# Scores by source parity, a transposed value sum, block-diagonal states, gate sums at odd tokens, and a new order

## The chip, the cores and the metric

One core of a Trainium2 chip runs the kernel. The metric is the device time of one execution in microseconds (us). The engines are TensorE (PE in the profile, with PEld for its weight loads), VectorE (DVE), ScalarE (ACT), GpSimd (POOL) and SyncE (SP), which here only issues transfers. Matmul results go to PSUM, which the kernel uses as eight banks of 128 x 512 float32; everything else lies in SBUF.

## What is computed

A gated linear attention over 4 batches, 8 heads, 768 tokens and head size 48, then a two-layer network over all 3072 tokens (384 to 2048 and back) with g = h * cos(h) in between.

```
f = 1.0 / (1.0 + np.exp(-f_logit))
for t in range(S):
    state = f[:, :, t, :, None] * state + np.einsum('bhd,bhe->bhde', k[:, :, t], v[:, :, t])
    y[:, :, t] = np.einsum('bhd,bhde->bhe', q[:, :, t], state)
x = np.ascontiguousarray(attn_out.transpose(0, 2, 1, 3)).reshape(B * S, H * D)
h = x @ w_in
g = h * np.cos(h)
return (g @ w_out).astype(np.float32)
```

## The kernel before

**Tiling.** The tokens are cut into 12 *pairs* of 256 tokens, n = 0 to 11, three pairs to a batch. In a pair, partition p holds two neighbouring tokens, the even one (e = 0) and the odd one (e = 1). The two halves of 64 partitions, g = 0 and 1, are two chunks of 128 tokens. Heads go in two groups of four, u = 0 and 1.

**Steps.** `describe` makes a graph of named steps; the number behind a name is the pair, and what follows the dot is a part of it:

- f, k, q, v: loads. ex and ln (ACT): softplus of -f_logit, the negative logarithm of the gate.
- cum (PE, L335 to L341): sums of it along the tokens of a chunk, once for each head group, for even and odd tokens alike (a 384-column matmul, two of 192 columns, one of them with a strict triangle as weights) and the chunk's total (four tiny matmuls). eb and ei (ACT): exponentials of minus and plus the sum.
- qm, km (L363, POOL or DVE): q times eb and k times ei. Both go through a transpose to qkt: pairs 0 to 3 on PE (tq, tk, L391, with the copy qkt), pairs 4 to 11 by a transposing DMA on SP's queue (tq, L380).
- sc (PE, L411): scores. The output's partitions are the source tokens of one parity x in the chunks g = 0 and 1, its columns the 128 targets. am (DVE, L415): mask.
- ps (PE, L434): the sum of k times v over a chunk. st (DVE, L449) adds the state that was carried, sz (L456) multiplies by the chunk's decay. The state is a tile of [128, 4, 2, 48] in which only the own half of the rows is filled, so that one matmul serves two heads.
- y (PE, L473): masked scores times v, a matmul for each head, parity and chunk, which contracts 64 tokens, with the scores as weights. yi (PE, L483): q times the state, added in the same PSUM.
- yb (copy), tx (PE, L505: three transposes), xe (copy): y is turned, so that x has the 384 features on partitions.
- vb: v in bf16. w, wc: weights loaded and cast to bf16, staged in the slots of g.
- h (PE, L531): first layer, for 128 tokens in units 0 and 1 and for 256 in units 2 to 12; co (ACT, L536): cosine; g (DVE, L513): product; o (PE, L547): second layer; ot: copy; out: store.
- zf (PE, L257): matmuls of zeros, which compute nothing.

**What sets the order.** `ORDER` (L34 to L110) is written out: every word is a step with its engine letter (T PE, S ACT, V DVE, G POOL, Y SP) and the slots of its tiles or PSUM banks. `emit` issues the steps in this order. Each engine runs its own steps in the order of the list and waits for the data. An activation of another kind than the one before costs a table load on ACT (L536, L586). `SLOTS` gives the number of buffers of each kind of tile.

Of the kernel before, what the change touches and what calls it, by code (L numbers as in the profile page):

```python
# [9 lines left out]
F32 = mybir.dt.float32  # L10
BF16 = mybir.dt.bfloat16
AF = mybir.ActivationFunctionType
HALF_PI = math.pi / 2.0

B, H, S, D = 4, 8, 768, 48
C = 128
# [4 lines left out]
HD = H * D  # L21
NQ = DF // 512
# [5 lines left out]
SLOTS = {"f": 3, "k": 3, "q": 3, "v": 3, "sp": 3, "b": 3, "bi": 3, "qk": 3, "vb": 3, "qkt": 5, "am": 4,  # L28
         "sz": 4, "st": 2, "yb": 4, "x": 4, "g": 5, "co": 4, "ot": 4}
WITHIN = 12  # L30
ZEROS = 24
# [3 lines left out]
zf0:T0 zsz.2:V zsp.2:V zqk.2:V zsp.0:V f0.1:S0 zf19:T1 zf21:T0 zf4:T4 zf18:T5 zf15:T4 zf11:T5  # L35
f1.0:S1 f0.0:S zqk.0:V zf8:T4 ex0.1:S ex1.0:S f1.1:Y zf17:T5 k0.1:Y0 ln1.0:S2 cum1.0:T2 eb1.0:S0
ln0.1:S0 cum0.1:T3 ex1.1:S k0.0:Y ex0.0:S ln0.0:S q1.0:Y0 qm1.0:G2 ln1.1:S ei0.1:S0 v0:Y0 tq1.0:T6
km0.1:V0 eb0.1:S1 k1.0:Y1 ei1.0:S1 km1.0:V zf14:T7 zf10:T1 cum0.0:T7 ei0.0:S km0.0:V tk1.0:T
cum1.1:T0 eb1.1:S qkt1.0:V0 q0.1:Y1 qm0.1:G eb0.0:S tk0.1:T1 f2:Y2 tq0.1:T qkt0.1:V1 q0.0:Y ex2:S
ln2:S0 q1.1:Y vb0:G0 ps0.1:T4,5 sc1.0:T2 am1.0:V0 ps0.0:T sc0.1:T6 am0.1:V1 tk0.0:T1 k1.1:Y qm0.0:G  # L40
tq0.0:T cum2.1:T2 sz0.00:V2 qm1.1:G ei1.1:S cum2.0:T qkt0.0:S2 sz0.01:V km1.1:G w0.0:Y0 wc0.0:G
zf6:T6 tq1.1:T7 tk1.1:T qkt1.1:S3 sc0.0:T0 sc1.1:T6 ei2:S2 eb2:S2 st0.1:V0 am0.0:V2 yi0.1:T4 zf12:T5
am1.1:V3 zf16:T0 sz0.10:V2 zsz.3:G v1:Y1 vb1:G1 sz0.11:V y0.0:T5 y0.1:T y1.1:T1,0 yb0.0:S0
ps1.0:T2,3 ps1.1:T y1.0:T yb0.1:V1 tx0.1:T6 w0.1:Y1 zf7:T7 yi1.0:T w0.2:Y2 tx0.0:T7 xe0.1:S0
st1.0:V1 h1.00:T4 sz1.00:V3 yb1.0:S2 zf20:T2 xe0.0:S sz1.01:V yi1.1:T w0.3:Y3 zf1:T1 w1.3:Y4 wc0.1:V
wc0.2:V k2:Y2 yb1.1:S3 zf2:T2 st1.1:V0 sz1.11:V2 wc0.3:V h1.01:T co1.0:S0 q2:Y2 zf13:T2 h0.10:T6
tx1.1:T1 wc1.3:G xe1.1:S1 sz1.10:G g1.0:V0 zqk.1:V km2.1:G0 qm2.1:G h0.01:T2 tx1.0:T0 h0.00:T
xe1.0:S qm2.0:G co0.0:S1 km2.0:G g0.0:V1 h0.11:T co0.1:S2 g0.1:V h1.10:T0 w1.2:Y2 h1.11:T co1.1:S3
h2.31:T4 h2.30:T co2.3:S0 h2.10:T2 h2.11:T h2.21:T6 g1.1:V tq2.1:T0 w1.1:Y3 wc1.1:G g2.3:V4 h2.20:T
co2.1:S1 tq2.0:T1 v2:Y2 g2.1:V wc1.2:V f3:Y0 o3.3:T4 tk2.1:T o1.3:T5 h2.01:T2 h2.00:T co2.2:S2  # L50
tk2.0:T g2.2:V co2.0:S3 qkt2.0:V4 w1.0:Y2 vb2:G2 wc1.0:G o1.2:T qkt2.1:S1 v3:Y0 g2.0:V o0.1:T6
o0.2:T ps2.1:T7 ps2.0:T sc2.0:T0 sc2.1:T2 st2.0:V1 o3.2:T o0.3:T ex3:S o1.1:T k3:Y0 am2.1:V2
am2.0:V1 sz2.01:V3 q3:Y1 f4:Y1 ln3:S2 yi2.0:T7 cum3.1:T2 sz2.00:G cum3.0:T o3.1:T ei3:S0 y2.1:T0
y2.0:T eb3:S1 f5:Y2 o0.0:T km3.1:V2 v4:Y1 km3.0:G qm3.1:G zf22:T1 q5:Y0 yb2.0:V1 vb3:S0 v5:Y2
tx2.0:T7 xe2.0:S2 yi2.1:T ps3.0:T1,2 ps3.1:T q4:Y2 qm3.0:V yb2.1:S0 sz3.00:V2 sz3.01:V tk3.0:T3
tq3.0:T qkt3.0:V2 ot0:S0 tk3.1:T7 out0:Y ex4:S tx2.1:T0 xe2.1:V o1.0:T ln4:S0 tq3.1:T ex5:S h3.11:T0
q6:Y1 ln5:S2 st3.1:V0 qkt3.1:V0 ot1:V1 o3.0:T ot3:V2 sz3.11:V3 sc3.1:T2 sc3.0:T6 k4:Y1 am3.1:V3
h3.10:T co3.1:S0 h3.30:T4 h3.31:T out1:Y am3.0:V0 co3.3:S1 g3.1:V3 h3.20:T2 f6:Y0 y3.0:T6,7 y3.1:T
yb3.0:S3 v6:Y0 yi3.1:T h3.21:T yb3.1:S2 k5:Y2 co3.2:S2 sz3.10:V h3.00:T0 tx3.1:T6 xe3.1:S3 h3.01:T
g3.3:V co3.0:S3 tx3.0:T7 xe3.0:V vb4:G1 g3.2:V cum4.1:T4 cum4.0:T ei4:S1 eb4:S0 h4.31:T6 h4.30:T  # L60
g3.0:V km4.1:G1 km4.0:G qm4.1:G h4.11:T2 h4.10:T o4.3:T0 co4.1:S0 h4.00:T4 g4.1:V2 co4.3:S1 g4.3:V
k6:Y0 o2.3:T1 h4.01:T co4.0:S2 o2.1:T qm4.0:G o4.0:T vb6:V2 o4.2:T vb5:V0 g4.0:V o4.1:T o2.2:T
cum5.1:T2 ot4:S3 cum5.0:T o2.0:T o5.3:T0 ei5:S2 tq4.1:Y3 o5.2:T eb5:S2 sc4.1:T6 ps4.1:T4,5 tq4.0:Y1
sc4.0:T2 ps4.0:T ot2:V0 km5.1:G0 qm5.1:G qm5.0:G am4.1:V2 o5.1:T st4.0:V1 km5.0:G ex6:S ln6:S0
o5.0:T ot5:V1 h4.20:T6 h4.21:T am4.0:V1 sz4.00:G2 f11:Y1 co4.2:S3 g4.2:V f8:Y2 out4:Y tq5.1:Y4
o7.3:T4 cum6.0:T0 yi4.0:T2 sz4.01:G cum6.1:T eb6:S1 o7.1:T y4.1:T3 y4.0:T o7.2:T ei6:S0 yb4.0:V1
yi4.1:T o7.0:T o6.3:T2 yb4.1:S0 st4.1:V0 sz4.10:G3 tx4.1:T5 tq5.0:Y0 ot7:S3 ex8:S sc5.0:T6 ps5.0:T3
ps5.1:T sc5.1:T0 qm6.0:V2 o6.2:T am5.0:V0 f7:Y0 tx4.0:T4 out5:Y am5.1:V3 k7:Y1 ex7:S o6.1:T km6.0:V
sz4.11:G ln7:S2 o6.0:T q8:Y2 xe4.1:S0 km6.1:V xe4.0:S h5.31:T6 h5.30:T h5.11:T0 st5.0:V1 sz5.01:G2
sz5.00:V h5.10:T h5.20:T4 h5.21:T co5.3:S0 g5.3:V1 co5.1:S1 g5.1:V yi5.0:T3 q7:Y0 h5.00:T6 co5.2:S2  # L70
g5.2:V h5.01:T co5.0:S3 k9:Y2 yi5.1:T0 y5.0:T y5.1:T yb5.1:S2 g5.0:V o8.1:T1 yb5.0:S3 o8.3:T
tx5.1:T0 tx5.0:T3 xe5.0:V1 tq6.0:Y2 xe5.1:V out3:Y qm6.1:G tq6.1:Y1 ot6:S1 ln8:S0 ps6.1:T4,5 ps6.0:T
sc6.0:T6 sc6.1:T2 am6.0:V2 sz6.01:V3 o9.0:T0 o9.2:T zsp.1:G h6.10:T6 v7:Y1 h6.11:T am6.1:V1 h6.21:T2
co6.1:S0 sz6.00:V st6.1:V0 sz6.10:G2 h6.20:T co6.2:S1 g6.1:V0 o9.1:T cum7.1:T4 cum7.0:T y6.1:T6,7
out2:Y y6.0:T f10:Y0 ex10:S g6.2:V vb7:V1 o8.2:T eb7:S0 yb6.0:S0 yi6.1:T qm7.0:G1 o9.3:T ei7:S1
o8.0:T h6.00:T2 ot9:V2 tx6.0:T0 yb6.1:V1 sz6.11:G tx6.1:T6 h6.01:T xe6.0:V2 out7:Y ot8:V0 k10:Y0
co6.0:S2 h6.30:T4 h6.31:T xe6.1:V h7.11:T0 g6.0:V h7.20:T6 co6.3:S3 h7.10:T co7.1:S0 h7.21:T km7.0:G
g6.3:V h7.01:T2 co7.2:S1 v8:Y0 vb8:V0 g7.1:V4 f9:Y2 h7.00:T co7.0:S2 km7.1:G h7.31:T4 h7.30:T
co7.3:S3 o10.0:T0 o10.2:T qm7.1:G g7.2:V o10.3:T g7.0:V v9:Y2 tq7.0:Y3 o10.1:T ex9:S sc7.0:T6
ps7.1:T1,2 tq7.1:Y0 out8:Y vb9:G2 ln9:S1 g7.3:V k8:Y1 ps7.0:T sc7.1:T4 o13.3:T3 o13.2:T ln10:S2  # L80
am7.0:V0 cum8.1:T6 cum8.0:T am7.1:V3 y7.1:T4,5 y7.0:T st7.0:V1 ei8:S2 sz7.01:V3 sz7.00:G st7.1:V0
km8.1:V0 o12.0:T1 eb8:S2 qm8.0:V yi7.0:T yb7.0:V2 qm8.1:V yi7.1:T yb7.1:S3 o13.1:T cum9.0:T6
# [575 lines left out]
```

## Time and profile before

| | us |
|---|---|
| median of 3 runs (lowest, highest) | 197.15 (196.1, 211.81) |
| span of the profiled execution | 193.8 |
| PE busy, L531 and L547 | 69.3 and 71.4 |
| DVE busy, L513 and L415 | 61.4 and 28.6 |
| ACT busy, L536 and its 20 table loads | 52.5 and 25.6 |
| POOL busy | 57.4 |
| read from and written to memory | 25.17 MB and 4.72 MB |

The span runs from the first to the last recorded instruction; a run's time holds a little more around it. Lines of groups show line, engine, operation, output<-inputs, shape and count, then busy time with the mean of one in ns, then the idle time before it and what ended that. Matmuls are pipelined, so the mean duration of one is not the distance to the next. Lines of a timeline begin with the start and the duration in us; where several alike are merged, the duration is that of all.

### The profile page before, as it was taken

What the parts mean: (1) busy time and instruction counts of PE and PEld (TensorE: products, weight loads), DVE (VectorE), ACT (ScalarE), POOL (GpSimd) and SP (SyncE); (2) the same over time, 40 slices, a digit from 0 to 9 for tenths busy, and PEclk for the clock granted to TensorE, in tenths of its full rate; (3) what the DMA queues carried; (4) which work ended last, traced back from release to release, by engine and by line L of the source; (5) the groups of instructions that cost most, each with busy time, mean ns of one, the idle gap of its engine ahead of it and who ended that gap; (6) DMA issues with size and microseconds to landing.
All of it is one profiled execution on the core that took longest, in us unless ns stands there. A gap on an engine that the chain in (4) does not pass through costs nothing.

```text
span 193.8 us, 5919 instructions
## 1 busy us (share of the span) xinstructions
PE 179.9 (93%) x2560; PEld 132.1 (68%) x2560; DVE 143.4 (74%) x194; ACT 137.3 (71%) x168; POOL 57.4 (30%) x75
## 2 busy tenths in 40 slices
PE   7377979998899999999979999999999999999995
PEld 2255658865678767677758867776776776777762
DVE  5069999994898278579965998589598789868420
ACT  3668668686799988988599896897575494446231
POOL 2249119405410727221017302724510540100000
PEclk9879999999999999999999999999999999999999
DMA  6999999779999899998990850499990024301213
GB/s 145 261 265 346 382 314 309 182 214 263 251 285 282 191 195 174 257 257 160 317 224 5 170 144 3 95 201 189 229 231 3 3 54 98 122 3 41 85 41 122
DMA packets 74106, 34.46 MB, mean 178 GB/s; under 512 B 67424, under 2 KB 72544, under 8 KB 74080
## 3 DMA queue, kind: packets, MB, share of 16 engines
q1 hardware_dynamic: 72496, 33.50, 72.6%
q10 hardware_dynamic: 1584, 0.59, 1.3%
q8 instruction: 20, 0.33, 0.7%
q14 instruction: 6, 0.05, 0.1%
HBM read 25.17 MB, written 4.72 MB: 154 GB/s over the span
## 4 chain that ended last, share of the span: by engine, by line
PE 72%; DVE 11%; ACT 8%; issue 4%; DMA 3%; POOL 1%; ACTq 0%; DVEq 0%; POOLq 0%
PE ps L547 29%; PE ps L531 27%; DVE w_in_bf L190 3%; PE ps L473 3%; DVE am L415 3%; DMA f<-in_f_logit_dram 3%; PE ps L411 2%; PE ps L483 2%; PE ps L335 2%; PE ps L505 2%; ACT f L321 2%; ACT sp L324 1%; DVE st L449 1%; PE ps L434 1%; DVE sz L456 1%
## 5 line engine op out<-in xcount | busy, mean ns | idle before, releaser
L513 DVE TENSOR_TENSOR g<-ps,co 128x1024 bf16<-128x1024 f32 x48 | 61.4, 1307 | 19.2 <-ACT co L536 19.1
L547 PE MATMUL ps<-w_out_bf,g 128*128 128x384 bf16 x384 | 71.4, 326 | 0.0
L531 PE MATMUL ps<-x,w_in_bf 128*128 128x256 bf16 (+1 forms) x624 | 69.3, 264 | 1.5 <-DVE w_in_bf L190 1.4
L536 ACT ACTIVATE co<-ps,halfpi 128x1024 bf16<-128x1024 f32 x48 | 52.5, 1114 | 21.1 <-PE ps L531 20.5
L531 PEld LDWEIGHTS <-w_in_bf 128*128 128x128 bf16 x624 | 56.4, 98 | 11.3 <-DVE w_in_bf L190 2.4
L547 PEld LDWEIGHTS <-g 128*128 128x128 bf16 x384 | 35.0, 98 | 19.7 <-issue 0.2
L415 DVE TENSOR_TENSOR am<-ps,pmask 128x1024 bf16<-128x1024 f32 x24 | 28.6, 1218 | 3.0 <-PE ps L411 2.8
L456 POOL TENSOR_TENSOR sz<-st,b 64x192 bf16<-64x192 f32 x20 | 11.1, 555 | 50.9 <-DVE st L449 49.7
L363 POOL TENSOR_TENSOR qk<-q,b 128x384 bf16<-128x384 f32 x18 | 18.2, 1021 | 15.3 <-DMA q<-in_q_dram 8.7
L363 POOL TENSOR_TENSOR qk<-k,bi 128x384 bf16<-128x384 f32 x15 | 15.4, 1033 | 18.6 <-ACT bi L354 13.3
L536 ACT ACT_TABLE_LOAD x10 | 12.8, 1283 | 4.4 <-PE ps L531 2.0
L363 DVE TENSOR_TENSOR qk<-k,bi 128x384 bf16<-128x384 f32 x9 | 8.1, 912 | 9.4 <-ACT bi L350 6.8
L586 ACT ACT_TABLE_LOAD x10 | 12.8, 1283 | 2.6 <-issue 2.4
L190 ACT COPY x<-ps 128x384 bf16<-128x384 bf16 x13 | 6.0, 478 | 9.2 <-PE ps L505 9.2
L321 ACT ACTIVATE f<-f 128x768 f32<-128x768 f32 (+1 forms) x14 | 10.3, 748 | 2.0 <-DMA f<-in_f_logit_dram 1.9
L335 PE MATMUL ps<-sp,incl 128*128 128x384 bf16 x24 | 8.2, 340 | 3.3 <-ACT sp L324 3.1
L354 ACT ACTIVATE bi<-ps 128x768 f32<-128x768 f32 x10 | 8.1, 812 | 3.7 <-PE ps L341 1.9
L257 PE MATMUL ps<-zero 128*128 128x512 bf16 x24 | 9.3, 493 | 1.4 <-DVE zero L196 1.2
L324 ACT ACTIVATE sp<-f 128x768 bf16<-128x768 f32 (+1 forms) x14 | 10.3, 749 | 0.3
L449 DVE TENSOR_TENSOR st<-ps,sz 128x384 f32<-128x384 f32 x16 | 8.9, 554 | 2.2 <-POOL sz L456 1.4
L411 PE MATMUL ps<-qkt 48*64 48x128 bf16 x384 | 9.2, 220 | 1.0 <-ACT qkt L190 0.8
L473 PE MATMUL ps<-vb,am 64*128 64x48 bf16 x384 | 7.4, 180 | 1.9 <-DVE g L513 1.1
(61 smaller groups left out, 174.9 us busy)
## 6 DMA issues: line engine op xcount, KB each, us to landing
v<-in_v_dram SPq DMA_DIRECT2D x12, 384.0 KB, 5.8
out_dram<-ot SPq DMA_DIRECT2D x24, 192.0 KB, 2.2
f<-in_f_logit_dram SPq DMA_DIRECT2D x10, 384.0 KB, 5.2
k<-in_k_dram SPq DMA_DIRECT2D x10, 384.0 KB, 5.9
q<-in_q_dram SPq DMA_DIRECT2D x10, 384.0 KB, 5.8
g<-in_moe_w_in_dram SPq DMA_DIRECT2D x4, 768.0 KB, 9.7
g<-in_moe_w_out_dram SPq DMA_DIRECT2D x4, 768.0 KB, 5.8
k<-in_k_dram SPq DMA_DIRECT2D x4, 192.0 KB, 5.0
```

The source lines that it names most:

```text
L321: nc.scalar.activation(out=flat(t.ap), in_=flat(t.ap), func=AF.Exp, scale=-1.0)
L324: nc.scalar.activation(out=s.ap[:, :, :, 0:D], in_=swap(t.ap), func=AF.Ln, bias=1.0)
L363: G.step(f"{nm}{n}.{u}", ("POOL", "DVE"), lambda e, u=u, j=j, src=src, dec=dec: eng(e).tensor_mul(out=qkp[u][j].ap[:, :, :, 0:D], in0=swap ...
L411: nc.tensor.matmul(o[t, r, 2 * a + x, :].rearrange("p (e n) -> p e n", e=2), lhsT=qkv(u)[s, 1, a, g, x, :], rhs=qkv(u)[s, 0, a, g, :, :], ...
L415: G.step(f"am{n}.{u}", ("DVE",), lambda e, u=u, sc=sc: nc.vector.tensor_mul(out=am[u].ap.rearrange("p r b n -> p (r b n)").rearrange("p (y ...
L456: eng(e).tensor_mul(out=new.ap[s, :, r, :].rearrange("p (u a) n -> p u a n", u=2), in0=ap()[s, :, r, :].rearrange("p (u a) n -> p u a n", ...
L473: nc.tensor.matmul(py[g].ap[:, D * i:D * i + D], lhsT=am[u].ap[t, h % 2, h // 2 * 2 + x, :], rhs=vb.ap[t, i, x, :], start=(py[g].first and ...
L513: nc.vector.tensor_mul(out=o.rearrange("p b (n e) -> p b e n", e=2), in0=ph.ap.rearrange("p (b e n) -> p b e n", e=2, n=64), in1=co.ap.rea ...
L531: nc.tensor.matmul(ph.ap[:, i * T:(i + 1) * T].rearrange("p (g t) -> p g t", t=C), lhsT=w_in_bf[:, kk, f0:f0 + 128], rhs=xa[:, :, kk, :], ...
L536: G.step(f"co{m}.{j}", ("ACT",), lambda e, ph=ph, co=co: nc.scalar.activation(out=co.ap, in_=ph.ap, func=AF.Sin, bias=halfpi), reads=[ph], ...
L547: nc.tensor.matmul(po.ap[:, 0:DM], lhsT=gT.ap[:, j, i * C:(i + 1) * C], rhs=w_out_bf[:, j, :], start=(po.first and j == 4 * s), stop=(po.f ...
L586: nc.scalar.preload_act_table_set("natural_log_exp_and_others")
```

## The change

1. **Gate sums at odd tokens only.** The sum over a pair of neighbouring tokens (ad, a new step on POOL or DVE; in pairs 0 and 1 PE adds them) replaces the sums for both parities. cum is one 384-column matmul for all eight heads in pairs 2 to 11, and two of 192 columns for each head group in pairs 0 and 1. eb and ei have half the elements. In exchange even tokens are corrected: fx (ACT) computes the odd tokens' gate, qa (DVE) multiplies the even tokens' q by 1 + exp(-f_logit), the inverse of it, and ka (POOL or DVE) the even tokens' k by the gate, both in place.
2. **Scores by source parity.** In sc the two source parities now fill the two halves of the output's partitions and the chunk goes into the columns, so am is [128 sources of a chunk, 128 targets] for each head and chunk. The mask changes to match.
3. **Value sum over 128 tokens, transposed.** vb is laid out by parity, and vt (four copies of 64 x 384 a pair, on DVE, POOL or ACT) puts the 128 tokens of a chunk on partitions, each head's 48 features with 16 zeros on each side. y multiplies am from the right: weights are 32 columns of vt, the output is 32 features by 128 targets; a head touches two such blocks. yi does the same with the state. The 32-row blocks of the output go round four column positions of the array. y comes out with features on partitions; yb, tx and the tile yb go away, and xe copies from PSUM to x.
4. **Block-diagonal states.** ps writes its two head parities to the two halves of the rows and the same columns. st is [128, 4, 48], made by two half-size steps, and sz writes the two diagonal blocks.
5. **Order and slots.** ORDER is new as a whole; there are 38 zf steps instead of 24, two slots ls and three vt. ex, ln, fx, eb and ei of two pairs often stand together, so ACT has 10 table loads instead of 20.

The diff, cut to its core:

```diff
-ZEROS = 24
+ZEROS = 38
...
-                for eq in range(2):
-                    nc.vector.tensor_copy(out=pmask[s, e, eq, :], in_=(strict if e > eq else incl)[s, s])
+                nc.vector.tensor_copy(out=pmask[s, e, :], in_=(strict if r > e else incl)[s, s])
...
+        def lead_q(e, t, w):
+            eng(e).scalar_tensor_tensor(out=w.ap[:, :, 0, :], in0=t.ap[:, :, 1, :], scalar=1.0, in1=w.ap[:, :, 0, :],
+                                        op0=ALU.add, op1=ALU.mult)
+        def gate_of(e, t, s):
+            nc.scalar.activation(out=t.ap[:, :, 0, :], in_=s.ap[:, 1, :, 0:D] if cut else s.ap[:, :, 1, :],
+                                 func=AF.Exp, scale=-1.0)
+        def lead_k(e, t, w):
+            eng(e).tensor_mul(out=w.ap[:, :, 0, :], in0=w.ap[:, :, 0, :], in1=t.ap[:, :, 0, :])
...
+            G.step(f"ad{n}", ("POOL", "DVE"), lambda e: eng(e).tensor_add(
+                out=sp.ap[:, 0, :, 0:D], in0=soft.ap[:, :, 0, :], in1=soft.ap[:, :, 1, :]), reads=[soft], writes=[sp])
...
-            nc.tensor.matmul(o4, lhsT=incl, rhs=w[:, 0:1, :, 0:D].broadcast_to([128, 2, 4, D]),
-                             start=True, stop=False)
-            nc.tensor.matmul(o4[:, 0], lhsT=strict, rhs=w[:, 1, :, 0:D], start=False, stop=False)
-            nc.tensor.matmul(o4[:, 1], lhsT=incl, rhs=w[:, 1, :, 0:D], start=False, stop=False)
+            for x in xe:
+                nc.tensor.matmul(o[:, :, 0:HB], lhsT=incl,
+                                 rhs=w[:, x, :, 0:D].rearrange("p (u h) d -> p u h d", u=un),
+                                 start=(x == 0), stop=False)
...
+        for j, (x, g) in enumerate(((0, 0), (1, 1), (0, 1), (1, 0))):
+            G.step(f"vt{n}.{j}", ("DVE", "POOL", "ACT"), lambda e, x=x, g=g: copy(
+                e, vt.ap[64 * x:64 * x + 64, H * g:H * g + H, 16:16 + D], vb.ap[64 * g:64 * g + 64, x]),
+                reads=[vb], writes=[vtp[j]])
...
-                                s, t = slice(64 * r, 64 * r + D), slice(64 * g, 64 * g + 64)
-                                nc.tensor.matmul(o[t, r, 2 * a + x, :].rearrange("p (e n) -> p e n", e=2),
+                                s, t = slice(64 * r, 64 * r + D), slice(64 * x, 64 * x + 64)
+                                nc.tensor.matmul(o[t, r, 2 * a + g, :].rearrange("p (e n) -> p e n", e=2),
...
+                        nc.vector.tensor_add(out=st.ap[s], in0=view()[s], in1=S0.ap[s, :, r, :])
+                    G.step(f"st{n}.{g}{r}", ("DVE",), carry, reads=[ps[g], S0], writes=[sts[r]])
...
+        def summed(work, ops):
+            lanes, left = [[w for w in work if w[1] % 4 == c] for c in range(4)], {}
...
+            for k in range(max(map(len, lanes))):
+                for w in (lane[k] for lane in lanes if k < len(lane)):
+                    g, b = w[0], w[1]
+                    c, m = b % 4, b // 4
...
+                    nc.tensor.matmul(py[g].ap[32 * c:32 * c + 32, C * m:C * m + C],
...
+                   lambda g, b, h, at: dict(lhsT=vt.ap[:, H * g + h, at:at + 32],
+                                            rhs=am[h // 4].ap[:, h % 2, h % 4 // 2 * 2 + g, :]))
...
-            G.step(f"tx{n}.{g}", ("PE",), turn, reads=[yb], writes=[px])
-            G.step(f"xe{n}.{g}", ("DVE", "ACT"), lambda e, g=g, o=o: copy(e, xg[g].ap, o()),
-                   reads=[px], writes=[xg[g]])
+            G.step(f"xe{n}.{g}", ("ACT", "DVE"), lambda e, g=g: copy(
+                e, xg[g].ap, py[g].ap[:, 0:DM].rearrange("p (m n) -> p m n", n=C)), reads=[py[g]], writes=[xg[g]])
```

Two lines of the new list, as an example of its form:

```
vt10.1:S2 ex10:S g8.1:V vt8.3:G0 km9.1:G vb9:G2 vt9.0:S1 ln10:S0 ex11:S ln11:S1 fx10:S
...
vt11.1:S sz11.01:V vt11.2:G vt11.0:G yi10:T0,1 y10:T y11:T6,7 yi11:T xe10.0:V1 xe10.1:S g10.1:V3
```

## The prediction

> **What bounds the kernel now.** First the page's head and its 40 slices, then the busy time in three stages, then the groups by line, then the timeline where a group starts and where two engines collide.
>
> ```profile
> PE 179.9 (93%) x2560; PEld 132.1 (68%) x2560; DVE 143.4 (74%) x194; ACT 137.3 (71%) x168; POOL 57.4 (30%) x75
> ```
>
> TensorE (PE) is busy in 93% of the span. I cut the span at two products of the list ORDER that both kernels have, g0.0 (in the trace at 31.5 us) and g9.3 (at 140.6), because the list can be read as time: when g9.3 starts, the list has issued 240 matmuls of L547 and 450 of L531, and the trace has started 240 and 457.
>
> ```profile
> core 0: us, PE busy (x) PEld busy (x) DVE busy (x) ACT busy (x) POOL busy (x), PEclk, DMA share, GB/s
> 0.00:31.50 31.50, 22.99 (x394) 15.77 (x395) 22.66 (x50) 20.41 (x34) 12.95 (x21) 0.95 1.08 287
> 31.50:140.60 109.10, 106.30 (x1559) 80.02 (x1557) 85.10 (x109) 90.42 (x103) 38.47 (x46) 1.00 0.88 198
> 140.60:193.80 53.20, 50.62 (x614) 36.29 (x611) 35.66 (x38) 26.46 (x32) 5.97 (x9) 1.00 0.27 73
> ```
>
> In the middle and last stage PE is full and VectorE (DVE) has a fifth or more free. In the first, PE waits for inputs and for ScalarE (ACT) and DVE.
>
> ```profile
> L505 PE MATMUL ps<-ident,yb 128*128 128x128 bf16 x72 | 7.3, 219 | 1.3 <-DVE yb L190 1.3
> L411 PE MATMUL ps<-qkt 48*64 48x128 bf16 x384 | 9.2, 220 | 1.0 <-ACT qkt L190 0.8 <-DVE qkt L190 0.2
> L363 DVE TENSOR_TENSOR qk<-k,bi 128x384 bf16<-128x384 f32 x9 | 8.1, 912 | 9.4 <-ACT bi L350 6.8 <-ACT vb L190 2.6
> L363 DVE TENSOR_TENSOR qk<-q,b 128x384 bf16<-128x384 f32 x6 | 3.6, 602 | 0.4 <-DMA q<-in_q_dram 0.4
> ```
>
> A matmul's mean is latency; what it costs is the distance between starts:
>
> ```profile
> 77.13 0.34 PE L335 MATMUL ps<-sp,incl 128*128 128x384 bf16 x1
> 77.30 0.25 PE L337 MATMUL ps<-sp,strict 128*128 128x192 bf16 x1
> 77.38 0.25 PE L338 MATMUL ps<-sp,incl 128*128 128x192 bf16 x1
> 77.47 0.24 PE L341 MATMUL ps<-half,sp 128*128 128x2 bf16 x4
> 77.57 0.81 PE L547 MATMUL ps<-w_out_bf,g 128*128 128x384 bf16 x4
> 78.31 0.58 PE L473 MATMUL ps<-vb,am 64*128 64x48 bf16 x32
> 78.82 0.82 PE L547 MATMUL ps<-w_out_bf,g 128*128 128x384 bf16 x4
> 79.57 0.36 PE L483 MATMUL ps<-sz,qkt 128*64 128x96 bf16 x8
> 79.87 0.50 PE L547 MATMUL ps<-w_out_bf,g 128*128 128x384 bf16 x2
> ```
>
> A cumulated sum costs 77.57 - 77.13 = 0.44 us, a value sum of 32 matmuls 0.51, eight state matmuls 0.30. Four matmuls of L547 cost 0.65 in the chain of waits, 0.75 here beside a small-tile group: 0.1 for each change of tile shape.
>
> **PE's stream.** Cumulated sums: 24 x 0.44 = 10.6; after 14, each with one 384-column matmul (0.17) or two of 192 (0.08) and four tiny ones (0.10): 14 x 0.27 = 3.8. Gain 6.8. Transposes of y (L505): the chain has six in 0.34, so 72 x 0.057 = 4.1 go, with their 24 yb copies. Value sum: 12 x 0.51 = 6.1 now; after, 384 matmuls of 32 output rows by 128 columns in four column lanes. No row has this shape. The nearest is L411, four tiles and 128 columns, 16 in 0.23 on the chain, 14 ns each; the other end is one at a time, as L505, 57 ns. I take 14, since L483's two column tiles already run at once (eight 96-column matmuls in 0.30): 12 x (32 x 0.014 + 0.1) = 6.6. State part: 14 groups of 0.30 and 6 of 0.28 = 5.9; after 240 x 0.014 + 12 x 0.1 = 4.6. Scores, outer sums, q/k transposes, L531 and L547 keep count and size. Net gain 6.8 + 4.1 - 0.5 + 1.3 = 11.7, by stage in us of PE (pricing each step of the list this way, L531 0.109 a matmul): first 12.1 before, 12.4 after; middle 104.4 and 94.5; last 49.3 and 47.4. The 14 more zero matmuls (0.215 each, 3.0 in all) lie in the first stage, where 19 us are not real work; uncovered they cost 3.
>
> **The other engines.** New on DVE or GpSimd (POOL): qa, ka, ad, vt, a split st. DVE prices: qa, ka, ad as L363's unhindered 0.55 (between 0.35, a 384-wide bf16 copy, and 0.91, the k row above); vt 0.27 (between 0.17, a 64x64 copy, and 0.35); st halves 0.35 as the 64x192 sz from PSUM, against one of 0.55. POOL: ka and ad 1.0 as its L363, vt 0.5 as its 64x192 sz. ACT: fx 0.48 as other 384-wide ones, eb and ei 0.48 for 0.81, 24 yb copies (16 of them ACT's) gone, 10 of 20 table loads of 1.28 gone. The middle stage by the list, before and after: ACT 94.7 and 90.9; DVE 90.8 and 100.1; POOL 34.0 and 76.6. The same prices against the measured 85.1 of DVE show that neighbours overlap by 6%, so DVE becomes 100.1 x 0.937 = 94: as much as PE, and POOL doubles.
>
> That matters because the two collide:
>
> ```profile
> 154.68 2.52 DVE L363 TENSOR_TENSOR qk<-k,bi 128x384 bf16<-128x384 f32 x1
> 154.83 1.96 POOL L363 TENSOR_TENSOR qk<-q,b 128x384 bf16<-128x384 f32 x2
> ```
>
> A DVE product of 0.55 took 2.52 while POOL ran two of its own; near 12 us two took 1.20 and 1.17; at 48.0 POOL's took 1.37 instead of 1.0 as DVE came first. What DVE reads from PSUM is not touched (yb at 48.45 beside POOL 0.55, as always), so L513 and the scores' mask are safe; products of two SBUF tensors are exposed. The Trainium skill, "SBUF — State Buffer", section "Who interferes with whom", has the rule: one SBUF port pair is shared under an exclusive lock, and a DVE instruction with two SBUF inputs and a GpSimd one that reads SBUF block each other for their whole length. These rows agree. In the middle stage 43 DVE instructions are exposed (qa 10, qm 7, km 2, ka 2, ad 4, vt 9, vb 1, sz from SBUF 8), and POOL is busy 76.6 of some 105 us, so about 32 meet it (no row shows a bf16 copy like vt beside POOL; a float one, w_in's at 28.31, kept its 1.75; without vt 25 meet it). Price of a meeting, from before: in its middle stage 22 exposed, 35% share, 8 meetings cost DVE 0.7 in all, 0.09 each; over the whole span 9 cost 3.9, 0.43 each; the two near 12 us 0.63. I take 0.2, between the first two: 6.4 us. Behind a blocked DVE instruction stand gate products (L513), which free the PSUM of L531; PE waits for those.
>
> SP issues the same number of loads, 16 transposes and 24 stores; ten inputs instead of eight precede the first weight, 0.79 MB at 287 GB/s = 2.7 us later, hidden while ACT is still at pairs 0 and 1. ACT's queue issues three loads at the start as now and two more later (f4, v11), at the 0.5 of SP's rows each.
>
> **The sum, in spans.** First stage: ACT gets 3 us more (24.5 by the list), but starts at 4.65 and would be done at 29.2, so I keep 31.5 (29.2 to 34.5). Middle: DVE 94 + 6.4, and 4.7 of waits as PE has now (109.1 - 104.4): 105. Last: 47.4 + 3.9 (now 53.2 - 49.3, with the last store) = 51.3. Span 31.5 + 105 + 51.3 = 187.8. The median run lies 197.15 - 193.84 = 3.3 above the span: 191.1.
>
> **Rivals.** *PE stays the bound*: collisions hit POOL or idle time, as most did so far; middle 94.5 + 4.7 = 99.2, span 182.0, time 185. For: 0.09 a meeting. Against: DVE has no slack left. *No change*: 0.43 a meeting, 13.8; middle 112.5, span 195.3, time 199. *Slower*: POOL's runs of six to eight instructions in the new list starve DVE, as at 154.68, while gate products wait; 32 x 0.63 = 20, middle 119, span 201.8, time 205; it decides from 0.5 a meeting up. Against: POOL feeds on DVE's results and runs dry. *The column lanes don't overlap*: 624 x (57 - 14) ns = 27, time 218. Against: L483. The Trainium skill speaks for it in "TensorEngine Tiling (Array Packing)", section "Tile-to-Partition Mapping": column tiling turns fast weight load off. Here L483's 64-column loads last 109 ns against 98 for full ones, yet its matmuls keep their pace.
>
> **How the numbers follow.** Forecast 191 (its own range 187 to 194) 0.42; PE-bound 185, 0.15; no change 0.22; slower 0.17; lanes serial 0.04. A measurement of this kernel tells 2% (193.2 and 201.1) from no change. Faster: 0.15 and six sevenths of 0.42 = 0.51. Same: 0.22 + 0.06 = 0.28. Slower 0.21. The range leaves out the lanes, half of slower and a few per cent below: 184 to 204.
>
> **What would show it.** Right: the value sum's 32 matmuls near 0.55 us; g9.3 near 136; DVE busier than 85 in the middle stage, and PE waiting there for L513's products. Wrong: qa, ad or vt rows with means over twice their price, or PE's small groups at 50 ns a matmul.

## The result and the profile after

| | before | after |
|---|---|---|
| median (lowest, highest), us | 197.05 (196.1, 211.81), 4 runs | 191.59 (190.05, 191.71), 4 runs |
| ratio, 95% interval | | 0.9734 (0.9682 to 0.9786) |
| span of the profiled execution, us | 193.8 | 189.9 |
| first, middle, last stage (cut at g0.0 and g9.3), us | 31.5, 109.1, 53.2 | 30.2, 108.8, 50.9 |

The changed kernel is 2.7% faster, 191.6 where 191 was forecast. Some executions of the same kernel take markedly longer (211.81 here); the ratios leave them out, the medians and highest values keep them. The stages tell a less comfortable story. The forecast had the middle stage fall from 109.1 to 105, and it fell by 0.3, which is no more than the spread: in a second profile of the old order (before_half_loads, below) that stage took 108.2. The gain of the two profiled spans, 3.9, lies in the last stage (2.3) and in the first (1.3).

The page's head and its row of the granted clock, after:

```profile
span 189.9 us, 5936 instructions
PE 173.3 (91%) x2510; PEld 124.1 (65%) x2512; DVE 152.3 (80%) x212; ACT 128.5 (68%) x180; POOL 95.0 (50%) x126
PEclk9979999999999996999999999999999999999999
```

PE lost 6.6 us of busy time, DVE gained 8.9 and POOL 37.6. The 6 in the clock row, the slice from 71.2 us, is new; it comes up below. The busy time by stage, after (first two numbers: the stretch and its length; then each engine's busy time and its instructions, the granted clock, the share of the DMA engines and GB/s):

```profile
core 0: us, PE busy (x) PEld busy (x) DVE busy (x) ACT busy (x) POOL busy (x), PEclk, DMA share, GB/s
0.00:30.20 30.20, 24.18 (x387) 14.90 (x389) 23.35 (x54) 21.73 (x40) 16.42 (x29) 0.94 1.09 286
30.20:139.00 108.80, 102.50 (x1630) 75.48 (x1627) 102.29 (x134) 86.67 (x116) 77.10 (x94) 0.98 0.96 212
139.00:189.90 50.90, 46.64 (x497) 33.75 (x496) 26.65 (x27) 20.13 (x25) 1.50 (x3) 0.99 0.17 55
```

In the middle stage DVE is busy 102.3 of 108.8 us, where it was busy 85.1 of 109.1: it is now as full as PE. In the page's chain of waits (share of the span, before and then after) PE's part is halved, DVE's is doubled, and no engine holds most of it any more:

```profile
PE 72%; DVE 11%; ACT 8%; issue 4%; DMA 3%; POOL 1%; ACTq 0%; DVEq 0%; POOLq 0%
```

```profile
PE 35%; DVE 24%; DMA 17%; POOL 7%; ACT 6%; issue 5%; SPq 3%; ACTq 1%; POOLq 0%; DVEq 0%
```

How its new instructions cost what they do is read from the groups by shape (after):

```profile
L394 DVE TENSOR_TENSOR qk<-q,b 128x384 bf16<-128x384 f32 x9 | 9.0, 999 | 1.4 <-ACT b L381 1.4
L336 DVE SCALAR_TENSOR_TENSOR q<-f,q 128x384 f32<-128x384 f32 x10 | 7.8, 783 | 0.2
L195 DVE COPY vt<-vb 64x384 bf16<-64x384 bf16 x12 | 6.5, 543 | 0.2
L521 PE MATMUL ps<-am,vt 128*32 128x128 bf16 x384 | 7.5, 220 | 2.7 <-DVE am L448 1.8 <-DVE sz L493 0.3 <-DVE vt L195 0.3
```

The shortest of these shapes in the same trace are 0.54 us for qm (L394), 0.52 for qa (L336) and 0.24 for vt. What the means of 1.00, 0.78 and 0.54 have above these comes from meetings with POOL. Duration above the shortest of the same shape, summed over DVE's instructions that read two SBUF tensors or copy one, comes to some 13 us in the execution and about 10 in the middle stage. It sits in few instructions: of the 41 such in the middle stage, 17 are longer than the shortest by over 0.1 us, each of them beside a POOL instruction, and these 17 hold nearly all of the 10, almost 0.6 each.

The value sum itself is as it was priced. The timeline of PE in a quiet stretch, after:

```profile
77.77 0.33 PE L364 MATMUL ps<-sp,incl 128*128 128x384 bf16 x1
77.93 0.24 PE L370 MATMUL ps<-half,sp 128*128 128x2 bf16 x4
78.10 0.42 PE L444 MATMUL ps<-qkt 48*64 48x128 bf16 x16
78.45 0.52 PE L521 MATMUL ps<-qkt,sz 128*32 128x128 bf16 x24
78.80 0.62 PE L521 MATMUL ps<-am,vt 128*32 128x128 bf16 x32
79.35 0.83 PE L569 MATMUL ps<-x,w_in_bf 128*128 128x256 bf16 x6
```

Starts tell the cost: a cumulated sum 78.10 - 77.77 = 0.33, the state part of a pair 0.35, the 32 matmuls of a value sum 79.35 - 78.80 = 0.55. The four column positions run at once: in the trace the matmuls of such a group start in fours, 2 to 5 ns apart, and the next four follow some 47 ns later.

What the collisions do to PE is seen once at full length (timeline of POOL, DVE and PE, after; the square bracket is the idle time before, and what ended it):

```profile
68.10 1.96 POOL L394 TENSOR_TENSOR qk<-q,b 128x384 bf16<-128x384 f32 x2
68.44 1.72 DVE L195 COPY vt<-vb 64x384 bf16<-64x384 bf16 x1
...
69.15 0.42 PE L444 MATMUL ps<-qkt 48*64 48x128 bf16 x16
...
70.20 2.51 DVE L551 TENSOR_TENSOR g<-ps,co 128x1024 bf16<-128x1024 f32 x2
...
71.56 0.42 PE L444 MATMUL ps<-qkt 48*64 48x128 bf16 x16 [1.99 <-DVE g L551]
...
71.91 4.34 PE L585 MATMUL ps<-w_out_bf,g 128*128 128x384 bf16 x16
```

A copy of 0.25 us (vt5.3) takes 1.72 while POOL runs two products back to back; behind it on DVE stand the gate products g3.3 and g4.3; the scores of pair 4 need the PSUM that g4.3 frees, so PE idles 1.99 us. Then its clock halves: the last line's 16 matmuls take 4.34 us, eleven of them starting 0.32 apart instead of the usual 0.163, which is eleven times 0.16, 1.7 us. That is the 6 in the clock row. Here a wait of 2 us cost nearly 4. It need not: in one of the experiments below (lanes_in_turn) PE waits equally long at the same place, and the same 16 matmuls take 2.77 us at full clock:

```profile
71.58 0.42 PE L444 MATMUL ps<-qkt 48*64 48x128 bf16 x16 [1.98 <-DVE g L551]
71.93 2.77 PE L585 MATMUL ps<-w_out_bf,g 128*128 128x384 bf16 x16
```

PE's longest waits in the middle stage, after (us in all, times, longest):

```profile
PE ps L444 <- DVE g L551: 2.0, 1, 2.0
PE ps L521 <- DVE am L448: 1.4, 1, 1.4
PE ps L569 <- DVE g L551: 0.9, 3, 0.4
```

All three are for DVE.

### The profile page after: what moved, and what is told of

Its sections match the earlier page's. It is cut to its first block, busy times and chain, and to the rows that moved or that the text cites. A ratio compares the mean times of both kernels' runs of the same rounds, so it can differ in the third digit from the quotient of the medians.

```text
span 189.9 us, 5936 instructions
## 1 busy us (share of the span) xinstructions
PE 173.3 (91%) x2510; PEld 124.1 (65%) x2512; DVE 152.3 (80%) x212; ACT 128.5 (68%) x180; POOL 95.0 (50%) x126
## 4 chain that ended last, share of the span: by engine, by line
PE 35%; DVE 24%; DMA 17%; POOL 7%; ACT 6%; issue 5%; SPq 3%; ACTq 1%; POOLq 0%; DVEq 0%
PE ps L585 18%; DVE g L551 11%; PE ps L569 11%; DMA k<-in_k_dram 7%; DMA v<-in_v_dram 6%; DVE am L448 3%; DVE q L336 3%; POOL qk L394 3%; DMA qkt<-qk 2%; DVE qk L394 2%; DMA out_dram<-ot 2%; PE ps L521 2%; POOL k L344 1%; PE ps L444 1%; SPq L413 1%
## 5 line engine op out<-in xcount | busy, mean ns | idle before, releaser
L585 PE MATMUL ps<-w_out_bf,g 128*128 128x384 bf16 x384 | 69.3, 332 | 0.0
L585 PEld LDWEIGHTS <-g 128*128 128x128 bf16 x384 | 36.5, 99 | 23.0 <-issue 1.3
L394 POOL TENSOR_TENSOR qk<-k,bi 128x384 bf16<-128x384 f32 x20 | 21.2, 1068 | 4.2 <-issue 3.3
L394 POOL TENSOR_TENSOR qk<-q,b 128x384 bf16<-128x384 f32 x15 | 15.6, 1049 | 8.2 <-DVE q L336 8.2
L344 POOL TENSOR_TENSOR k<-k,f 128x384 f32<-128x384 f32 (+1 forms) x12 | 11.1, 926 | 7.5 <-DMA k<-in_k_dram 6.3
L195 POOL COPY vt<-vb 64x384 bf16<-64x384 bf16 x24 | 13.2, 552 | 2.0 <-POOL qk L394 0.6
L195 DVE COPY ot<-ps 128x384 f32<-128x384 f32 x8 | 4.4, 552 | 10.5 <-PE ps L585 10.5
L487 DVE TENSOR_TENSOR st<-ps,sz 64x192 f32<-64x192 f32 x32 | 11.2, 352 | 1.6 <-PE ps L521 0.6
L195 ACT COPY ot<-ps 128x384 f32<-128x384 f32 x16 | 7.3, 476 | 6.9 <-PE ps L585 4.8
L195 ACT CAST x<-ps 128x384 bf16<-128x384 f32 x14 | 6.4, 479 | 6.9 <-DVE x L195 5.1
L336 DVE SCALAR_TENSOR_TENSOR q<-f,q 128x384 f32<-128x384 f32 (+1 forms) x14 | 9.2, 656 | 1.4 <-ACT f L328 1.2
L394 DVE TENSOR_TENSOR qk<-q,b 128x384 bf16<-128x384 f32 x9 | 9.0, 999 | 1.4 <-ACT b L381 1.4
L444 PEld LDWEIGHTS <-qkt 48*64 48x64 bf16 x384 | 6.3, 106 | 5.8 <-issue 3.1
```

What stands on the lines that cost most here:

```text
L195: (nc.scalar.copy if e == "ACT" else eng(e).tensor_copy)(out=o, in_=i)
L336: eng(e).scalar_tensor_tensor(out=w.ap[:, :, 0, :], in0=t.ap[:, :, 1, :], scalar=1.0, in1=w.ap[:, :, 0, :], op0=ALU.add, op1=ALU.mult)
L344: eng(e).tensor_mul(out=w.ap[:, :, 0, :], in0=w.ap[:, :, 0, :], in1=t.ap[:, :, 0, :])
L394: G.step(f"{nm}{n}.{u}", ("POOL", "DVE"), lambda e, u=u, j=j, src=src, dec=dec: eng(e).tensor_mul(out=qkp[u][j].ap[:, :, :, 0:D], in0=swap ...
L444: nc.tensor.matmul(o[t, r, 2 * a + g, :].rearrange("p (e n) -> p e n", e=2), lhsT=qkv(u)[s, 1, a, g, x, :], rhs=qkv(u)[s, 0, a, g, :, :], ...
L585: nc.tensor.matmul(po.ap[:, 0:DM], lhsT=gT.ap[:, j, i * C:(i + 1) * C], rhs=w_out_bf[:, j, :], start=(po.first and j == 4 * s), stop=(po.f ...
```

## The experiments

Explanations to be told apart for the middle stage: DVE, with its work and its blocked time, is the bound (A in the expectations); PE's stream still is (B); the transfers are, whose engines are busy 0.96 of that stage (C). Beside these, whether the port that DVE and POOL meet on, or only the amount of DVE's work, is what counts. All edits are to the changed kernel unless said otherwise, and each ratio is against the kernel before, run on the same chip (it is not the quotient of the medians shown).

| run | median us (lowest, highest) | ratio (95%) | span |
|---|---|---|---|
| the change | 191.59 (190.05, 191.71) | 0.9734 (0.9682 to 0.9786) | 189.9 |
| vt_dve_to_act | 191.52 (190.63, 192.45) | 0.9806 (0.9692 to 0.992) | 190.4 |
| vt_pool_to_act | 196.88 (195.95, 197.61) | 1.0045 (0.9999 to 1.0092) | 195.0 |
| cum_five_times | 194.43 (192.59, 195.87) | 0.9912 (0.9849 to 0.9975) | 190.9 |
| lanes_in_turn | 195.21, one run | | 193.4 |
| half_loads | 191.5 (190.32, 191.65) | 0.973 (0.9669 to 0.979) | 189.9 |
| before_half_loads | 196.45 (194.53, 196.89) | 0.9988 (0.9957 to 1.0018) | 194.7 |
| no_qa | 188.52 (186.94, 189.13) | 0.9586 (0.9522 to 0.9649) | 186.2 |
| half_loads_no_qa | 190.93 (189.76, 194.17) | 0.9701 (0.9625 to 0.9777) | 192.4 |
| no_pool_vt | 190.4 (190.0, 191.28) | 0.97 (0.9664 to 0.9736) | 189.4 |
| vt5_later | 191.86 (190.82, 193.95) | 0.9806 (0.9756 to 0.9856) | 189.0 |
| two_moves | 192.72 (191.28, 194.67) | 0.9808 (0.9765 to 0.9851) | 189.5 |
| sum_on_pe | 188.88 (188.51, 189.04) | 0.9578 (0.9551 to 0.9606) | 187.1 |

### vt_dve_to_act: DVE's twelve vt copies go to ACT

```diff
-... sz0.00:V vt0.0:V km1.0:V ...
+... sz0.00:V vt0.0:S km1.0:V ...
(and so for the other eleven words vtN.j:V)
```

> The 12 vt copies of DVE go to ACT; nothing else changes. They keep DVE busy 6.5 us (9 of them, 4.6 us, in the stage from g0.0 to g9.3), 3.5 us of it waiting for POOL. Theory A (DVE with its collisions bounds the middle stage): the middle stage shrinks from 108.8 to 104-106, time 187 to 189.5. Theory B (PE still bounds it, as before): DVE's time is free, time 191 to 192. If ACT were the bound: slower by up to 4.

Measured: 191.52, no gain. The middle stage, and the longest of PE's waits in it:

```profile
29.40:139.60 110.20, 102.03 (x1629) 75.45 (x1626) 95.72 (x125) 91.23 (x125) 75.95 (x94) 0.98 0.96 211
```

```profile
PE ps L444 <- DVE am L448: 1.9, 1, 1.9
PE ps L521 <- ACT vt L195: 1.4, 1, 1.4
PE ps L364 <- ACT ot L195: 1.3, 1, 1.3
PE ps L444 <- ACT ot L195: 1.1, 1, 1.1
```

DVE did lose 6.6 us in this stage (102.3 to 95.7) and the stage did not shorten. Of PE's listed waits 5.2 us stood on DVE and 0.4 on ACT; now it is 3.3 and 4.3. ACT issues nine more copies in this stage and comes late to vt and to the copies of the output (ot) behind them. So the sum of DVE's work is not by itself the bound: in a list written for one division of work, each engine in turn is late somewhere. That last step is a reading of the waits; no run tests it alone.

### vt_pool_to_act: POOL's 24 vt copies go to ACT

```diff
-... zvt.0:G vt0.1:G2 zsz.2:G ...
+... zvt.0:G vt0.1:S2 zsz.2:G ...
(and so for the other 23 words vtN.j:G)
```

> The 24 vt copies of POOL go to ACT (13.2 us of POOL, 19 of them in the middle stage); DVE's own instructions are the same. Theory A with collisions: POOL's share of the middle stage falls from 71% to 61%, DVE's waits for it from 9.8 us to 7-8, time 188.5 to 190.5, unless ACT (86.7 of 108.8 busy, plus 10) becomes late. Theory B: 191 to 192.

Measured: 196.88, the whole gain of the change gone. The middle stage, and its first wait:

```profile
31.60:143.90 112.30, 102.30 (x1630) 75.95 (x1628) 99.49 (x133) 95.83 (x135) 66.11 (x75) 0.98 0.94 203
```

```profile
PE ps L521 <- ACT vt L195: 3.6, 2, 2.7
```

ACT is busy 95.8 and is late twice for the value sum, 3.6 us in all; the first stage lost 1.4 too. This run cannot say what POOL's copies cost on the port, since ACT's lateness covers it; no_pool_vt below asks that.

### cum_five_times: four more matmuls ahead of each cumulated sum

```diff
+            for _ in range(0 if cut else 4):
+                nc.tensor.matmul(o[:, :, 0:HB], lhsT=incl,
+                                 rhs=w[:, 0, :, 0:D].rearrange("p (u h) d -> p u h d", u=un),
+                                 start=True, stop=True)
```

> The first matmul of cum runs five times in pairs 2 to 11 (four repeats are overwritten): 40 more PE matmuls of 0.162 us, 6.5 us, of which 5.2 in the middle stage and 1.3 before it. Theory A (PE has slack there): +0.5 to +3 us, time 192 to 194.5. Theory B (PE is the bound): +5 to +6.5, time 196.5 to 198.

Forty more matmuls at 0.163 are 6.5 us of PE, 32 of them in the middle stage. Measured: 2.8 more in the median, 1.0 more in the profiled span (this execution kept the full clock in every slice, the one of the change lost 1.7 to half clock).

```profile
29.80:140.10 110.30, 105.52 (x1662) 77.74 (x1659) 98.59 (x134) 87.00 (x116) 77.72 (x94) 1.00 0.98 212
```

With the half clock set aside, the 6.5 cost 2.7 in the profiled execution and up to 4.5 in the median; only the rest disappears in time that PE waits anyway. PE is not the whole bound of this stage, but it has no more than a few us of slack. DVE's part is as telling: with the same instructions it is busy 98.6 here instead of 102.3, and its time above the shortest is 5.9 instead of 10. How many instructions meet depends on the moment at which each comes, and the stage got longer although DVE's meetings got fewer.

### lanes_in_turn: the column positions one after the other

```diff
-            for k in range(max(map(len, lanes))):
-                for w in (lane[k] for lane in lanes if k < len(lane)):
+            for lane in lanes:
+                for w in lane:
```

> y and yi issue all blocks of one column position, then those of the next, so that neighbours in the queue share a position. If only different positions run at once: 56 ns a matmul instead of 14, 12 value sums of 1.8 us instead of 0.55, in all +20 to +26 us of PE; time 205 to 216, less what PE's waits absorb. If 32-column weights are what makes it fast, whatever the position: 191 to 192.

Measured: 195.21, 3.6 more, and not the 20 and more that a full loss of the overlap would cost. In the chain of waits the same 56 matmuls (24 of state, 32 of value sum) are one piece in both kernels; the change, and then lanes_in_turn:

```profile
78.52 0.90 PE ps L521 x56
```

```profile
77.25 1.78 PE ps L521 x56
```

That is 16 ns each when the position changes with every matmul, 32 ns in the mean when neighbours share one. The runs on one position are not strictly one after the other: in the timeline the first matmuls of the value sum start between the last of the state part, behind which they are issued. At 0.88 a pair the edit adds some 10 us of PE, for 3.6 more of time, or about 5 if the 1.7 of half clock is set aside here too: slack of the same kind as in cum_five_times. It is one execution.

### half_loads and before_half_loads: q and v of the later pairs fetch half

```diff
+        few = name[0] in "qv" and "." not in name and int(name[1:]) >= 4 and name != "v9"
+        h1 = h0 + 4 if few else h1
...
-            out=val.ap.rearrange("p h e d -> p h (e d)"),
+            out=val.ap[:, 0:h1 - h0].rearrange("p h e d -> p h (e d)"),
```

> The loads of q and v of pairs 4 to 11 (but v of pair 9) fetch four of eight heads; the other heads keep old data, every instruction of the engines stays. 15 x 512 packets of 384 bytes less, at 27 ns each on 16 engines 13 us of DMA time. Theory C (the DMA engines, 96% busy in the middle stage of the changed kernel, now bound it): that stage shrinks by 6 to 13 us, time 179 to 186. Theory A (engines in their written order, DVE first): time 190 to 192, within 1 us of the changed kernel.

> The same shorter loads (here of all 16 loads of q and v of pairs 4 to 11) in the kernel before, whose DMA engines are 88% busy in the middle stage and whose PE has 106 of 109 us of work there. Theories A and C both say that PE bounds it: 196 to 197.5. Below 194, the loads had held it up as well.

The edit leaves v9 whole in both kernels, so 15 loads are shorter in each. Measured: 191.5 and 196.45, both as without the edit. The middle stage of half_loads:

```profile
29.70:139.00 109.30, 102.10 (x1630) 75.50 (x1628) 101.04 (x133) 86.30 (x116) 76.84 (x94) 0.98 0.83 186
```

The transfers' share fell from 0.96 to 0.83 and the stage did not shorten. They are not the bound, in either kernel. C falls.

### no_qa: the correction of q left out from pair 4 on

```diff
         def lead_q(e, t, w):
+            if n >= 4:
+                return
```

> qa, the DVE product for even tokens' q, is left out of pairs 4 to 11 (that correction of the output is missing); nothing takes its place. 8 instructions, 6 to 7 us of DVE with their waits for POOL, and POOL's qm no longer waits for them (7.2 us in the middle stage). Theory A: middle stage -4 to -6 us, time 185.5 to 188. Theory C: 190.5 to 192.

Measured: 188.52, 3.1 less than the change; the direction is A's, the size below what A gave. The middle stage (g0.0 at 29.6, g9.3 at 135.4):

```profile
29.90:135.30 105.40, 100.23 (x1628) 74.56 (x1625) 96.26 (x125) 85.83 (x116) 74.99 (x94) 1.00 1.00 221
```

DVE lost about as much busy time here, 6.0, as in vt_dve_to_act, and this time, with nothing handed to another engine, the stage lost 3.0. The time above the shortest of each shape is 7.6 in this stage, from about 10, and no slice has half clock, so the 3.0 hold three things at once: eight products of some 0.55, fewer meetings, and the clock.

### half_loads_no_qa: both edits

> Both edits at once. If DVE alone bounds the middle stage: as no_qa, 185.5 to 188. If the DMA engines alone do: as half_loads. If the two bound it together: below both by at least 2 us, 176 to 184.

Measured: 190.93, not below no_qa, with a spread of 4.4 us. None of its four executions is below 189.7, so the 176 to 184 of a common bound did not come. Whether the edits hinder each other can't be told from executions that differ so much; the profiled one is the longest of them.

### no_pool_vt: fifteen of POOL's vt copies left out

```diff
-            G.step(f"vt{n}.{j}", ("DVE", "POOL", "ACT"), lambda e, x=x, g=g: copy(
+            G.step(f"vt{n}.{j}", ("DVE", "POOL", "ACT"), lambda e, x=x, g=g: None if e == "POOL" and n in (
+                4, 5, 6, 7, 8, 10, 11) else copy(
```

> 15 of the POOL copies vt (pairs 4 to 8, 10 and 11) are left out, so parts of v keep old values; DVE's, ACT's and PE's instructions stay. POOL has 8.3 us less to do. Collision theory: DVE's waits for POOL in the middle stage, 9.8 us at a POOL share of 71%, fall in proportion to 63%, by 1 to 2 us; time 189.5 to 191. If POOL's own length bounds the stage: 183.5 to 187. If neither: 191 to 192.

Measured: 190.4, 1.2 less, within what the port theory gave, but the intervals of the two ratios overlap. DVE does the same work as in the change, and its time above the shortest is about 8 in the middle stage instead of about 10. But half_loads and cum_five_times, in which POOL and DVE do all their work, have about 9 and 5.9, and the middle stage is as long as in the change, 108.75 (g0.0 at 29.80, g9.3 at 138.55). So this run shows no effect of POOL's copies that can be told from none.

### vt5_later and two_moves: the exposed instruction moved

The copy that collided at 68.44 is moved behind the gate products that waited for it; two_moves also puts am9.1 ahead of qa11 and qm10.1.

```diff
-... g4.2:V vt5.3:V g3.3:V g4.3:V o4.1:T0
+... g4.2:V g3.3:V g4.3:V o4.1:T0
...
-... vt4.1:V o4.2:T ...
+... vt4.1:V vt5.3:V o4.2:T ...
```

> One word of the list moves: the DVE copy vt5.3, which stood 1.72 us behind two POOL products at 68.4 us, between two gate products, now comes after vt4.1, some 6 us later. All work stays. Collision theory (a blocked DVE instruction holds the gate products behind it, and PE waits for those): the 1.5 us, PE's wait of 2.2 us and the half clock that followed it (11 matmuls at 320 instead of 163 ns, 1.7 us) go, time 188.5 to 190.5. If DVE's amount of work alone counts: 191 to 192.

> Beside vt5.3, the mask am9.1 moves ahead of qa11 and qm10.1, two DVE products that met POOL at 129 us and made PE wait 1.4 us for am9.1. Collision theory: another 0.5 to 1.5 us, time 187.5 to 190. If only the amount of work counts: 191 to 192. If the transpose of pair 10, which now starts 1.2 us later, is urgent: above vt5_later.

Measured: 191.86 and 192.72, no gain. The wait at 70 is gone: g4.3 starts at 67.8 instead of 71.4. But five us later (timeline of vt5_later):

```profile
73.14 1.94 POOL L394 TENSOR_TENSOR qk<-k,bi 128x384 bf16<-128x384 f32 x2
73.31 2.18 DVE L353 TENSOR_TENSOR sp<-ls 128x384 bf16<-128x384 f32 x1
75.55 0.32 PE L364 MATMUL ps<-sp,incl 128*128 128x384 bf16 x1 [2.91 <-DVE sp L353]
```

The next exposed instruction, the pair sum ad, starts 0.17 us behind POOL, is blocked through two products, and PE waits 2.91 us for it; the clock halves after that too. A wait cured by a move in the list came back as the next meeting of the same kind. In two_moves PE's wait for am9.1 falls from 1.4 to 0.3 as intended, the 2.91 is there as well, and the middle stage takes 109.0.

### sum_on_pe: the pair sum goes back to PE

vt5_later, and the step ad is dropped: ln writes both parities into sp as pairs 0 and 1 already do, and cum adds them with two matmuls. The zeroing of the sp tiles moves to the start, and the slots follow.

```diff
-        soft = None if cut else Val(lsS)
...
-            o, i = (s.ap[:, :, :, 0:D], swap(t.ap)) if cut else (flat(s.ap), flat(t.ap))
+            o, i = s.ap[:, :, :, 0:D], swap(t.ap)
...
-        if not cut:
-            G.step(f"ad{n}", ("POOL", "DVE"), ...
...
-        xe = (0, 1) if cut else (0,)
+        xe = (0, 1)
```

> vt5_later, and beside it ad (the sum over two neighbouring tokens, 5 on DVE, 5 on POOL) leaves the vector engines: PE adds both parities in cum, as it does in pairs 0 and 1. DVE 3.1 and POOL 5.0 us less, PE 10 x (0.162 + 0.10) = 2.6 us more, and cum follows ln directly. Theory that DVE and POOL on their common port bound the middle stage, and that a stall removed at one instruction goes to the next exposed one (ad, in vt5_later): time 187.5 to 190. Theory that PE's own work bounds it: 192.5 to 194.5. Theory that every engine's written order holds the others, so that no single relief shows: 191 to 192.5.

Measured: 188.88, the fastest complete kernel of the study, 4.2% below the kernel before; its interval (0.9551 to 0.9606) lies clear of that of the change (0.9682 to 0.9786). The middle stage, about (g0.0 is at 29.1, g9.3 at 135.9, so 106.8), and the page's clock row:

```profile
29.90:136.00 106.10, 101.72 (x1663) 75.58 (x1660) 97.28 (x130) 85.88 (x116) 70.76 (x89) 1.00 0.99 219
```

```profile
PEclk9999999999999999999999999999999999999999
```

```profile
PE ps L562 <- DVE g L544: 1.0, 3, 0.4
PE ps L437 <- DVE am L441: 0.9, 1, 0.9
```

Ten matmuls of 0.163 on PE and forty tiny ones (1.6 us, and 1.0 by the expectation) replace ten sums on DVE and POOL, which read two SBUF tensors each. No wait of PE in this stage is above 1.0, and the clock stays full in every slice. How much of the 2.0 in the middle stage is the clock and how much DVE's 5 us is not separated. The totals give a hint: one execution of half_loads, which is as fast as the change, kept the full clock and took 190.3, and the four of sum_on_pe with a mean clock of 0.998 and more took 188.5 to 188.9. So of the 2.7 between the medians some 1.5 is not the clock, as far as one execution on another chip tells.

## Why the prediction was right, and where not

The total, 191 against 191.59, is right partly by luck, because errors of opposite sign met: first stage 1.3 and last stage 0.4 too high, middle stage 3.8 too low, the addition behind the span 1.5 too high. Of the four signs of being right, three came; the fourth, g9.3 near 136, did not: it starts at 139.0.

- **PE's stream.** Right. The value sum takes 0.55, as priced, and the state part 0.35 a pair against 0.38; a cumulated sum takes 0.33 where 0.27 was taken, 0.6 us in ten. The rival in which the column lanes don't overlap is refuted by the trace (16 ns a matmul in the mixed group), and lanes_in_turn shows what some 10 of its 27 us would have done.
- **DVE becomes the bound.** Right in the main: 85.1 to 102.3 busy, PE's longest waits are for DVE, and no_qa and sum_on_pe, which take work from DVE without giving it to ACT, gain. Without the excess DVE's 102.3 would be about 92, where 94 was taken. Two qualifications come from the runs: PE is only a few us behind (in cum_five_times DVE was busy 3.7 less and the stage still grew by 1.5 with PE's added work), and DVE's load can't be handed over for nothing (vt_dve_to_act). So DVE with its meetings is not the bound alone.
- **The collisions.** This is the term of the sum that was mis-sized, in both factors. The prediction took 32 meetings at 0.2, 6.4 us; the trace has 17 instructions that are longer by over 0.1, at almost 0.6 each, about 10 us. The 32 came from multiplying the exposed instructions by POOL's share, and the price of 0.09 from dividing by such a product (22 exposed at a share of 35%); counted in the rows, the middle stage of before has two lengthened instructions, not eight, at 0.37 each. A price near 0.6 a meeting is the one that the prediction gave to its rival *slower*. That the count was too high while the price was too low kept the term from being off by more, which is luck. How long a meeting lasts is not one number. The 1.72, the 2.18 and, before, the 2.52 us are waits through two of POOL's products; elsewhere DVE gets in after one, as in the lines below, and the POOL product behind it takes 1.31 instead of 1.0. The doubt whether a bf16 copy is exposed is settled: vt's mean is 0.54 against 0.25 alone, just at twice its price, the sign of trouble that the prediction named. The Trainium skill, "SBUF — State Buffer", section "Who interferes with whom", counts copies among the operations that can enter the shared port's two-port modes; vt agrees with that. The lines (after):

```profile
129.34 1.19 POOL L394 TENSOR_TENSOR qk<-k,bi 128x384 bf16<-128x384 f32 x1
129.60 1.35 DVE L394 TENSOR_TENSOR qk<-q,b 128x384 bf16<-128x384 f32 x1
130.50 1.31 POOL L394 TENSOR_TENSOR qk<-q,b 128x384 bf16<-128x384 f32 x1
```

- **The waits.** 4.7 were taken over from before. DVE now idles 108.8 - 102.3 = 6.5, and one thing behind these that was not in the sum is the half clock after PE's longest wait, 1.7 us of PE in this execution. With the DVE work 1.7 lower, the collisions 3.6 higher and the waits 1.8 higher, the 105 becomes the 108.8 that was measured.
- **The last stage.** 51.3 forecast, 50.9 measured. PE's list fell by 1.9 there and DVE was far from full; a stage that is bound by one engine gave back about what that engine lost. The profiles agree on it: 53.2 and 53.3 before, 50.8 to 51.2 in all the others but lanes_in_turn.
- **The first stage.** Kept at 31.5, it took 30.2. In before DVE waited 6.8 us there for the exponential of L350 and PE 3.1 for ACT's softplus; in after DVE's longest wait for ACT's exponentials is 1.4 and PE's for the softplus 0.3. The forecast counted ACT's work and not who waited for it; that this is the cause was not tested, and before_half_loads, with 33.2, shows that this stage varies by more than the 1.3.
- **From span to median.** The 3.3 were two things. Every execution, of either kernel, has a time 1.8 above its span; the other 1.5 was that the profiled execution of before was a short one. before_half_loads, whose transfers make no difference, has stages 33.2, 108.2 and 53.3 in its profile: its first stage is 1.7 longer. Adding that 1.5 to a forecast of the new kernel was not justified.
- **The rivals.** PE-bound (185) fell by the collisions. No change (199) and slower (205) had the mechanism and prices of 0.43 and 0.63 a meeting, which are near what a meeting cost (0.6; single ones reached 1.5 to 1.6); what they had wrong was the count of 32. In the middle stage the measured 108.8 lies halfway between the 105 of the forecast and the 112.5 of no change: PE was relieved of 9.9 us by the list and the stage became 0.3 shorter.
- **Left open.** Whether the 38 zero matmuls cost anything, what the ten table loads less are worth, and how much of the result is the new order and how much the new products was not tried. What starts the half clock is open too.

## What to carry to other kernels

When work leaves a full engine, cut the profile into stages and ask in each which engine is full next: here 9.9 us off PE's list bought 0.3 where DVE filled up, and 1.9 bought 2.3 where it had room. Work that is spread over DVE and GpSimd to balance them should be priced with the other one running: count in a trace the rows that are lengthened and take their price from those rows (here 17 at almost 0.6), not from an average over all that might meet. It can be cheaper to put such work back on a matmul. Judge a move by its stage and not by the sum of one engine's busy time, for in lists that are issued in order the wait you remove can reappear at the next exposed instruction.

## What the runs showed that was not expected

- A wait of PE of 2.0 us (after) was followed by a half granted clock that held to about 76 us, the starts of L585 going from 0.163 to 0.32; vt5_later shows it after a wait of 2.91, and no_pool_vt after one of 1.23 (half clock from 57.1). Each of these three stretches lasted 3.4 us. In lanes_in_turn a wait of 1.98 was not followed by one, so the length of the wait alone does not settle it. The Trainium skill, "TensorE: Matmul & The Clock Gate", section "HAM oscillation — how this bites in real kernels", gives gaps over some 3.4 us as the ones to avoid; here shorter ones were followed by half clock, though not every time.
- DVE can lose to two of POOL's products in a row: 1.72 for a copy of 0.25, 2.18 for a sum of 0.56. In the row at 129.60 it got in between two.
- Not every conversion is exposed: the float to bf16 cast of the first weights on DVE (128 x 1536) took 1.75 in both kernels, in before beside a busy POOL, while the bf16 copy of 64 x 384 goes from 0.25 to 0.54 in the mean.
- Matmuls of 32 output rows whose neighbours share a column position took 32 ns each in the mean, against 16 when the position changes every time; fully serial they were expected at 56.
